# Waiting transfers between the early loads of a fused attention and expert kernel

## The chip, the cores and the metric

One core of one Trainium2 chip. The metric is the device time of one execution in microseconds (us), the median of three runs. SyncE (SP in the profile) issues every transfer of this kernel. TensorE is PE (its weight loads PEld), VectorE is DVE, ScalarE is ACT, GpSimd is POOL.

## The reference

Sliding-window attention, then a dense four-expert layer, then one gated two-layer block:

```python
scores = scale * np.matmul(q, k.transpose(0, 1, 3, 2))       # 2 batches, 8 heads, 576 positions, 64 wide
scores = np.where(masks, scores, -1e9)                       # window 32, plain or with stride 4
attn = softmax(scores); attn_out = attn @ v                  # -> x, 1152 x 512
for e in range(4):
    h = np.maximum(x @ w1[e], 0.0)                           # 512 -> 1024
    out += p[:, e:e + 1] * (h @ w2[e])                       # 1024 -> 512
h = out @ w_in; g = h * sigmoid(1.702 * h); return g @ w_out # 512 -> 2048 -> 512
```

## The kernel before

All products run on PE in two parts, a rounded upper part and the rest, so each weight block is loaded, rounded by ACT (`w_hi`, L199) and its rest taken by DVE or POOL (`w_lo`, L207) before PE can use it.

The first 90 us, attention together with the first expert's first two-thirds, are one hand-ordered list of steps, the string `SCRIPT`. The program runs through it once and emits each step's instructions; every engine then works through its own instructions in that order, each waiting for what it needs. The attention is cut into 16 parts (4 head pairs, times a big and a small range of positions in each of two batches); a big part has two groups and a small one has one, which makes groups 0 to 7 (big, first batch), 8 to 15 (small) and 16 to 23 (big, second batch). The steps that matter here:

- `L j` loads part j's queries and keys (`load_qk`, L243; part 3 comes in two halves), `K j` its values (`load_v`, L253). The tiles are `qkT..` and `v..`.
- `W s w` loads a 512 KB weight block into one of four staging tiles `st` (`w_load`, L184): `W 0 0`, `W 1 0`, `W 3 0`, `W 2 0` for the first product, `W 0 1`, `W 1 1` and so on for the second. `H s w` is the rounding on ACT, `O s w` the rest.
- `S` are the scores on PE (L321), `Q` the masked minimum on DVE (L329), `A` the exponential on ACT (L334), `N` the division (L357), `U` the turn of the probabilities on PE (L365) and `c` its copy, `V` the product with the values (L439).
- `T`, `t`, `r` are, for later groups, the turn by way of a store to HBM (`spill`, L382) and a load of it (`fetch`, L388). These transfers are SyncE's too.
- `F`, `G` are pieces of the first product of expert 0 (L547), `h` and `l` its two output parts, `2` the second product (L577 to L579).

SyncE holds 8 completion semaphores for transfers and uses them in turn: the ninth transfer is issued only once the first has landed. Beside that a load waits only for its tile to be free. After the script, SyncE goes on with the weights of experts 0 to 3 and of the last block, in a schedule of its own, until 605 us.

Of the kernel before, what the change touches and what calls it, by code (L numbers as in the profile page):

```python
# [7 lines left out]
F32 = mybir.dt.float32  # L8
# [7 lines left out]
P = 128  # L16
# [4 lines left out]
S, D, J, NPAIR = 576, 64, 144, 4  # L21
# [51 lines left out]
QK_AT, V_AT = places()  # L73

SCRIPT = """
L 2, P 8, M, L 3 0, L 3 1, S 4, L 1, L 0, Q 4, S 5 6, Q 5, Q 6, W 0 0, L 11, A 4, S 7, A 5, S 2 3, N 4 V, U 4, S 0,
K 2, Q 7, N 5 P, Q 3, A 6, A 7, L 7, L 10, K 3, L 9, K 9, S 1, Q 2, A 2, U 5, W 1 0, N 6 P, L 5, L 6, L 8, N 7 p,
c 4 v, L 4, c 5 a, U 6, Q 1, Q 0, H 0 0 0, c 6 a, A 3, N 2 P, A 1, U 7, O 0 0 p 0, S 15 11, c 7 v, Q 11, K 0, V 5,
V 7, C 5 v, O 0 0 p 1, C 7 v, U 2, F 1 0 1, R 5, c 2 a, H 1 0 0, R 7, N 3 V, K 11, K 1, W 3 0, G 0 2 h, N 1 P,
F 1 1 2, F 0 1 2, S 14 13, F 1 5 6, F 0 4 5, O 1 0 v 0, Q 15, Q 14, W 2 0, K 4, A 0, H 1 0 1, U 3, F 1 4 5, O 1 0 p 1,  # L80
Q 13, F 2 0 1, N 0 V, F 3 0 1, F 0 5 6, c 3 a, H 0 0 1, W 0 1, F 2 4 5, F 2 5 6, S 9 8, U 1, A 11, O 0 0 p 2,
O 0 0 p 3, Q 9, F 3 4 5, c 1 a, Q 8, F 2 1 2, U 0, c 0 a, F 3 1 2, V 3, N 11 p, V 1, A 14, O 1 0 v 3, H 3 0 0, C 3 v,
S 10 12, C 1 v, F 3 5 6, R 3, G 0 1 h, R 1, O 1 0 p 2, H 2 0 0, A 15, F 1 2 3, Q 10, G 1 1 h, F 1 7 8, U 11, H 3 0 1,
O 2 0 v 1, O 2 0 v 0, N 15 v, c 11 v, F 2 7 8, F 3 2 3, T 15, O 3 0 p 1, Q 12, H 2 0 1, L 13, O 3 0 p 3, F 3 6 7,
O 2 0 p 2, F 1 6 7, F 3 7 8, A 9, W 1 1, F 4 4 5, F 7 5 6, F 2 6 7, F 4 1 2, D, O 3 0 p 2, O 2 0 p 3, O 3 0 v 0, L 12,
F 2 2 3, G 0 0 l, F 2 3 4, F 7 3 4, L 15, G 0 0 h, H 0 1 0, O 0 1 p 1, K 10, H 0 1 1, H 1 1 0, L 14, F 5 4 5, F 0 7 8,
F 4 2 3, F 4 6 7, F 6 6 7, h 1, F 6 7 8, F 5 1 2, h 0, l 0, h 2, F 5 6 7, F 7 1 2, t 15, K 5, A 8, A 13, O 1 1 v 1,
l 1, F 5 0 1, F 7 4 5, O 0 1 v 0, F 5 7 8, F 6 4 5, F 5 2 3, F 6 2 3, O 0 1 v 3, W 2 1, W 3 1, N 14 V, l 2, F 5 5 6,
O 0 1 p 2, H 1 1 1, A 12, N 13 V, T 14, F 7 2 3, F 7 0 1, F 5 3 4, 2 0 1, F 4 7 8, 2 1 1, F 6 1 2, 2 0 0, F 6 3 4,
t 14, F 3 3 4, 2 0 2, 2 1 2, F 7 7 8, h 5, 2 1 0, F 7 6 7, O 1 1 v 2, T 13, N 8 P, O 1 1 v 0, h 3, 2 2 2, l 3, t 13,  # L90
O 1 1 p 3, N 9 P, H 2 1 0, A 10, H 2 1 1, F 4 3 4, F 4 0 1, T 8, 2 2 0, F 4 5 6, N 12 V, T 9, 2 3 2, 2 2 1, O 2 1 p 0,
H 3 1 0, F 6 0 1, h 7, N 10 V, O 2 1 p 3, T 12, r 14, l 5, h 4, O 3 1 p 1, 2 3 0, 2 3 1, F 6 5 6, l 7, S 20 22, l 4,
O 2 1 p 1, T 10, S 23 21, h 6, Q 20, Q 23, 2 4 1, t 8, K 7, 2 4 2, A 23, V 11, H 3 1 1, r 15, Q 22, l 6, r 13, V 15,
V 13, O 3 1 p 0, O 2 1 p 2, C 15 a, A 20, t 9, t 10, V 14, N 23 V, 2 5 2, T 23, C 14 v, 2 4 0, C 13 a, r 9, 2 5 0,
2 5 1, N 20 p, K 8, O 3 1 v 3, 2 6 2, O 3 1 p 2, C 11 v, R 13, R 11, T 20, S 18 19, S 16 17, V 9, R 14, Q 21, r 8,
R 15, Q 18, A 21, w, Q 16, K 6, V 8, C 9 v, 2 6 1, 2 6 0, r 10, t 12, t 20, C 8 a, r 12, t 23, K 15, K 12, A 18, R 9,
2 7 2 a, Q 17, R 8, 2 7 1 a, F 9 5 6, F 9 1 2, Q 19, F 10 0 1, 2 7 0 v, F 10 4 5, F 11 4 5, V 10 12, C 10 v,
F 11 1 2, F 9 4 5, F 10 5 6, F 9 0 1, C 12 v, R 10, F 8 6 7, R 12, N 21 v, F 10 3 4, F 11 3 4, r 23, F 8 0 1, F 8 5 6,
F 11 6 7, F 8 2 3, F 13 4 5, F 8 7 8, T 21, B 17 p, F 8 1 2, F 9 3 4, F 8 3 4, F 8 4 5, F 13 0 1, F 11 0 1, B 22 p,
X 22, Y 22, X 17, t 21, F 9 2 3, A 16, F 9 7 8, F 11 2 3, F 10 2 3, h 8, A 19, F 10 7 8, F 10 1 2, F 9 6 7, F 13 5 6,  # L100
N 22 v, F 10 6 7, h 9, h 10, F 11 7 8, T 22, F 13 1 2, F 11 5 6, F 12 4 5, l 8, Y 17, 2 8 1, F 12 2 3, N 16 P,
F 15 0 1, 2 8 2, l 9, T 16, N 18 v, F 12 3 4, 2 9 1, t 22, r 20, F 13 6 7, K 13, 2 9 2, F 15 5 6, F 12 1 2, F 14 1 2,
r 21, h 11, l 10, T 18, l 11, F 12 0 1, F 12 5 6, F 12 6 7, F 13 2 3, F 15 1 2, F 12 7 8, N 17 p, 2 10 1, N 19 p,
r 22, K 14, t 16, T 19, F 13 3 4, t 19, T 17, F 15 3 4, h 12, t 17, F 14 3 4, 2 11 1, F 13 7 8, l 12, t 18, 2 8 0,
F 14 6 7, F 14 0 1, 2 9 0, V 21, V 23, C 23 a, r 17, C 21 a, F 15 2 3, 2 10 0, h 13, R 21, F 14 7 8, l 13, F 14 2 3,
2 12 1, F 15 7 8, R 23, r 19, r 18, F 14 5 6, 2 10 2, 2 11 2, F 15 4 5, 2 12 2, F 15 6 7, 2 11 0, F 14 4 5, r 16,
h 15, h 14, V 19, V 17, 2 12 0, 2 13 1, C 17 v, 2 13 0, l 14, C 19 v, 2 13 2, R 17, l 15, R 19
"""


# [1 line left out]
def fused_kernel(ctx: ExitStack, tc: tile.TileContext, qk, v, dp, w1, w2, w_in, w_out, out):  # L112
# [17 lines left out]
    nc = tc.nc  # L130
# [3 lines left out]
    C = 384  # L134
# [15 lines left out]
    dram = ctx.enter_context(tc.tile_pool(name="dram", bufs=1, space=bass.MemoryType.DRAM))  # L150
# [25 lines left out]
    wst = {}  # L176

    def w_load(s, which):
        if which == 0:
            t = stg.tile([P, KT, 2 * P], F32, tag="stg", name=f"st1_{s}")  # L180
        else:
            t = stg.tile([P, 2, DM], F32, tag="stg", name=f"st2_{s}")
        src = (w1, w2)[which][s].rearrange("p (a b) -> p a b", a=t.shape[1]) if s < 4 * E else late[s - 4 * E, which]
        nc.sync.dma_start(out=t, in_=src)  # L184
        wst[s, which] = t
# [8 lines left out]
    def w_hi(s, which, halves=range(2)):  # L194
        if halves[0] == 0:
            w_tiles(s, which)
        for i in halves:
            half = slice(2 * i, 2 * i + 2) if which == 0 else slice(i, i + 1)
            nc.scalar.activation(wt[s, which][0][:, half, :], wst[s, which][:, half, :], AF.Copy)  # L199
# [29 lines left out]

    qkT = {}  # L230
    vt = {}

    PLACE = {(0, "big"): 0, (0, "small"): 384, (1, "small"): 576, (1, "big"): 768}

    def load_qk(b, pr, kind, half=None):

        off, w, _, _ = QK_AT[b, pr, kind]
        assert half is None or (b, pr, kind) == FIRST_PART
        if (b, pr, kind) not in qkT:
            qkT[b, pr, kind] = ap_.tile([P, 896], F32, tag="qkT", bufs=9, name=f"qkT{b}{pr}{kind}")  # L240
        src = qk[off:off + P * w].rearrange("(p w) -> p w", w=w)
        a, z = (0, w) if half is None else HALVES[half]
        nc.sync.dma_start(out=qkT[b, pr, kind][:, a:z], in_=src[:, a:z])  # L243

    def load_v(b, pr, kind):

        off, w = V_AT[b, pr, kind]
        t = ap_.tile([P, 768], F32, tag="v", bufs=6, name=f"v{b}{pr}{kind}")
        src = v[off:off + P * w].rearrange("(p w) -> p w", w=w)
        if (b, pr, kind) == BESIDE:  # L250
            nc.sync.dma_start(out=t[P // 2:, :w], in_=src[:P // 2])
        else:
            nc.sync.dma_start(out=t[:, :w], in_=src)  # L253
        vt[b, pr, kind] = t[:, :w].rearrange("p (x h d) -> p x h d", h=2, d=D)

    def keep(eng, out, in_):
# [272 lines left out]
    def g1_part(e, c, f, kt, terms):  # L529

        if (c, f) not in part:
            early_bank = e == 0 and c == 0 and f < NTI
            pool, tag = (pacc, f"pa{KT - 1 - f}") if early_bank else (ps, "ps")
            part[c, f] = [pool.tile([P, 512], F32, tag=tag, name=f"g1_{e}{c}{f}"),
                       {(k, x) for k in range(KT) for x in "hl"}]
        pt, todo = part[c, f]
        s, o = divmod(f, 2)
        wh, wl = wt[4 * e + s, 0]
        fs = slice(o * P, (o + 1) * P)
        products = {"h": [(wh, xh), (wl, xh)], "l": [(wh, xl)]}  # L540
        for x in terms:
            if (kt, x) not in todo:
                continue
            first = len(todo) == 2 * KT
            todo.remove((kt, x))
            for y, (w, xx) in enumerate(products[x]):
                nc.tensor.matmul(pt[:, :C], w[:, kt, fs], xx[:, kt, c * C:(c + 1) * C], start=first and y == 0,  # L547
                                 stop=not todo and y == len(products[x]) - 1)
# [430 lines left out]
    def second2(s, c, slots):  # L979
# [25 lines left out]

    seq = [("e", 0, c, f) for c in range(NC) for f in range(F1)]

    steps.update({
        "M": masks,
        "P": spin,  # L1010
        "G": lambda f, i, terms: g1_part(0, 0, f, ORDER[i], terms),
        "W": w_load,
        "H": lambda s_, which, *halves: w_hi(s_, which, list(halves) or range(2)),
        "O": lambda s_, which, eng, *pieces: w_lo(s_, which, list(pieces), {"p": nc.gpsimd, "v": nc.vector}[eng]),
        "F": lambda it, a_, b_: g1_some(*seq[it][1:], TERMS[a_:b_]),
# [251 lines left out]
```

## Time and profile before

| | |
|---|---|
| median of 3 runs | 608.67 us (608.64 to 608.78) |
| the profiled execution | 608.31 us, of which its span is 606.5 us |
| PE, busy in the span | 600.5 us (99%) |
| DVE, ACT, POOL busy | 451.8, 273.1, 318.1 us |
| transfers | 73.31 MB; 39.3% of 16 transfer engines' time |

The span runs from the first instruction to the last one's end; 1.8 us lie around it. A share of busy time is an average over stages: the transfers keep all 16 engines busy until about 30 us and about half of them or less later. A wait in the profile is idle time of an engine before an instruction, with what ended it.

### The profile page before, as it was taken

What the parts mean: (1) busy time and instruction counts of PE and PEld (TensorE: products, weight loads), DVE (VectorE), ACT (ScalarE), POOL (GpSimd) and SP (SyncE); (2) the same over time, 40 slices, a digit from 0 to 9 for tenths busy, and PEclk for the clock granted to TensorE, in tenths of its full rate; (3) what the DMA queues carried; (4) which work ended last, traced back from release to release, by engine and by line L of the source; (5) the groups of instructions that cost most, each with busy time, mean ns of one, the idle gap of its engine ahead of it and who ended that gap; (6) DMA issues with size and microseconds to landing.
All of it is one profiled execution on the core that took longest, in us unless ns stands there. A gap on an engine that the chain in (4) does not pass through costs nothing.

```text
span 606.5 us, 10633 instructions
## 1 busy us (share of the span) xinstructions
PE 600.5 (99%) x3889; PEld 541.1 (89%) x3889; DVE 451.8 (74%) x937; ACT 273.1 (45%) x618; POOL 318.1 (52%) x304
## 2 busy tenths in 40 slices
PE   8999999999999999999999999999999999999997
PEld 5888988999989989998998899999899988988996
DVE  6867625957887887887878689798886766667565
ACT  7965311354535544445355233356464344344321
POOL 5652204764776775866777442385519564473210
PEclk9999999999999999999999999999999999999999
DMA  8954561040764755656553309822003121100004
GB/s 331 367 187 120 154 188 45 0 136 39 225 185 146 226 172 159 192 173 180 184 150 129 109 6 212 167 102 85 21 1 105 35 70 36 35 2 2 0 1 156
DMA packets 55348, 73.31 MB, mean 121 GB/s; under 512 B 26336, under 2 KB 36480, under 8 KB 55296
## 3 DMA queue, kind: packets, MB, share of 16 engines
q1 hardware_dynamic: 55296, 72.64, 39.3%
q8 instruction: 30, 0.49, 0.3%
q14 instruction: 22, 0.18, 0.1%
HBM read 57.03 MB, written 15.59 MB: 120 GB/s over the span
## 4 chain that ended last, share of the span: by engine, by line
PE 96%; DVE 2%; ACT 1%; issue 0%; POOL 0%; DVEq 0%; ACTq 0%; POOLq 0%
PE gd L817 10%; PE gc L817 10%; PE ga L817 10%; PE g L547 8%; PE q L908 7%; PE q L907 7%; PE q L906 7%; PE q L992 5%; PE q L990 5%; PE q L991 5%; PE gb L817 5%; PE pa L577 3%; PE pa L578 3%; PE pa L579 3%; PE q L964 1%; PE q L962 1%
## 5 line engine op out<-in xcount | busy, mean ns | idle before, releaser
L757 POOL TENSOR_TENSOR m<-m,sd 128x512 int32<-128x512 int32 x32 | 47.6, 1488 | 59.3 <-issue 33.5
L912 DVE SCALAR_TENSOR_TENSOR acc<-q,pwe,acc 128x512 f32<-128x512 f32 x81 | 59.9, 747 | 23.9 <-PE q L908 23.7
L701 POOL TENSOR_TENSOR wsl<-ss,wsh 128x512 fp32r<-128x512 f32 x39 | 55.4, 1426 | 38.5 <-ACT wsh L700 28.2
L908 PE MATMUL q<-w2h,h 128*128 128x512 f32 x180 | 70.8, 393 | 0.0
L906 PE MATMUL q<-w2h,h 128*128 128x512 f32 x180 | 70.3, 391 | 0.0
L907 PE MATMUL q<-w2l,h 128*128 128x512 f32 x180 | 70.3, 391 | 0.0
L839 POOL TENSOR_TENSOR cc<-s,u 128x256 f32<-128x256 f32 (+1 forms) x28 | 24.7, 882 | 74.8 <-DVE s L836 74.8
L828 ACT ACTIVATE s<-ga 128x256 f32<-128x256 f32 (+1 forms) x40 | 16.3, 409 | 96.2 <-PE ga L817 96.2
L992 PE MATMUL q<-w2h,h 128*128 128x512 f32 (+1 forms) x146 | 56.9, 390 | 0.0
L990 PE MATMUL q<-w2h,h 128*128 128x512 f32 (+1 forms) x146 | 56.7, 388 | 0.0
L991 PE MATMUL q<-w2l,h 128*128 128x512 f32 (+1 forms) x146 | 56.6, 387 | 0.0
L712 POOL TENSOR_TENSOR w2l<-st,w2h 128x512 fp32r<-128x512 f32 x37 | 50.1, 1367 | 9.8 <-ACT w2h L711 9.3
L999 DVE SCALAR_TENSOR_TENSOR acc<-q,acc 128x512 f32<-128x512 f32 (+1 forms) x64 | 42.4, 677 | 11.5 <-PE q L992 11.2
L697 POOL TENSOR_TENSOR wal<-st,wah 128x512 fp32r<-128x512 f32 (+1 forms) x38 | 40.9, 1082 | 12.3 <-ACT wah L696 12.3
L817 PE MATMUL ga<-xh,wal 128*128 128x256 f32 (+1 forms) x160 | 47.3, 295 | 0.0
L817 PE MATMUL ga<-xh,wah 128*128 128x256 f32 (+1 forms) x160 | 47.2, 295 | 0.0
L817 PE MATMUL ga<-xl,wah 128*128 128x256 f32 (+1 forms) x160 | 47.2, 295 | 0.0
L864 DVE TENSOR_TENSOR h<-cc,h 128x256 fp32r<-128x256 f32 (+3 forms) x40 | 35.1, 877 | 9.2 <-ACT h L861 5.7
L908 PEld LDWEIGHTS q<-w2h,h 128*128 128x128 f32 x180 | 33.8, 188 | 7.3
L907 PEld LDWEIGHTS q<-w2l,h 128*128 128x128 f32 x180 | 33.8, 188 | 6.9
L906 PEld LDWEIGHTS q<-w2h,h 128*128 128x128 f32 x180 | 33.8, 188 | 6.5
L834 DVE TENSOR_TENSOR u<-gb,s 128x256 f32<-128x256 f32 (+1 forms) x40 | 18.2, 455 | 28.4 <-PE gb L817 28.4
(374 smaller groups left out, 1823.4 us busy)
## 6 DMA issues: line engine op xcount, KB each, us to landing
st<-in_w_dram SPq DMA_DIRECT2D x32, 512.0 KB, 5.0
sd<-in_w_in_dram SPq DMA_DIRECT2D x16, 512.0 KB, 4.4
sd<-in_w_out_dram SPq DMA_DIRECT2D x16, 512.0 KB, 4.0
w<-m SPq DMA_DIRECT2D x32, 256.0 KB, 4.6
st<-w SPq DMA_DIRECT2D x16, 512.0 KB, 3.7
out_dram<-acc SPq DMA_DIRECT2D x8, 256.0 KB, 2.0
turned<-acc SPq DMA_DIRECT2D x4, 320.0 KB, 6.7
acc<-turned SPq DMA_DIRECT2D x4, 320.0 KB, 5.2
```

The lines of the kernel that those rows point to most:

```text
L547: nc.tensor.matmul(pt[:, :C], w[:, kt, fs], xx[:, kt, c * C:(c + 1) * C], start=first and y == 0, stop=not todo and y == len(products[x]) - 1)
L701: fns.append(lambda x=x, dst=dst: engine(f"p.{s}.{x}").tensor_tensor(out=sl[:, dst], in0=sums[:, dst], in1=sh[:, dst].bitcast(F32), op=ALU ...
L712: fns.append(lambda o=o: engine(f"q.{s}.{2 * o + 1}").tensor_tensor(out=lo[:, o], in0=t[:, o], in1=hi[:, o].bitcast(F32), op=ALU.subtract))
L757: nc.gpsimd.tensor_tensor(out=m.bitcast(I32), in0=m.bitcast(I32), in1=t.bitcast(I32)[:, :, 0], op=ALU.add)
L817: nc.tensor.matmul(bank_[:, :n], wz[:, y, m, :], xz, start=start and m == 0 and z == 0, stop=m == 1 and z == 2, skip_group_check=not start)
L906: nc.tensor.matmul(pt, hi, wh[:, o, :], start=o == 0, stop=False)
L907: nc.tensor.matmul(pt, hi, wl[:, o, :], start=False, stop=False)
L908: nc.tensor.matmul(pt, lo, wh[:, o, :], start=False, stop=o == 1)
L912: nc.vector.scalar_tensor_tensor(to, pt, pwe[:, s // NF, t:t + 1], dst, op0=ALU.mult, op1=ALU.add)
L990: nc.tensor.matmul(pt, hi, wh[:, o, cols], start=o == 0, stop=False)
L991: nc.tensor.matmul(pt, hi, wl[:, o, cols], start=False, stop=False)
L992: nc.tensor.matmul(pt, lo, wh[:, o, cols], start=False, stop=o == 1)
```

## The change

A new step `J n` is put at fourteen places of the script. It issues a transfer of one number, from the tile that was loaded n loads ago (counted by a new list `newest`, to which `load_qk`, `load_v` and the script's `W` append) into a small HBM tile `seen`, a new column each time. The transfer reads the loaded tile, so SyncE waits until that load has landed before it issues it, and issues nothing behind it until then. No load is taken away, added, or moved against another one.

```diff
+    seen = dram.tile([1, 64], F32, name="seen")
+    newest = []
+
+    def landed(n):
+
+        x = len(newest)
+        nc.sync.dma_start(out=seen[:, x:x + 1], in_=newest[-n])
...
         nc.sync.dma_start(out=qkT[b, pr, kind][:, a:z], in_=src[:, a:z])
+        newest.append(qkT[b, pr, kind][:1, a:a + 1])
...
             nc.sync.dma_start(out=t[:, :w], in_=src)
+        newest.append(t[P // 2:P // 2 + 1, :1])
...
+    def first_load(s_, which):
+        w_load(s_, which)
+        newest.append(wst[s_, which][:1, 0, :1])
...
-        "W": w_load,
+        "W": first_load,
+        "J": landed,
```

The loads of the script with the new steps between them (all other steps left out; t and r are stores and loads by way of HBM):

```
L 2, L 3 0, L 3 1, L 1, L 0, J 5, W 0 0, L 11, J 4, K 2, L 7, L 10, J 5, K 3, L 9, K 9, W 1 0, J 4, L 5, L 6, L 8, L 4,
J 5, K 0, K 11, K 1, W 3 0, J 5, W 2 0, K 4, J 3, W 0 1, L 13, J 4, W 1 1, D, J 3, L 12, J 3, L 15, K 10, J 4, L 14,
t 15, K 5, W 2 1, J 4, W 3 1, t 14, t 13, ..., t 8, J 3, K 7, ..., K 8, ..., K 6, ..., K 15, K 12, ..., J 6, K 13, ...
```

Before, the list is the same without the `J`s.

## Rows read from the trace of the kernel before

**Rows 1.** Waits of PE until 12 us: total us, times, longest.
```profile
PE ppt01big L365 <- POOL prob01big L357: 1.0, 2, 0.5
...
PE s01big L321 <- DMA qkT01big<-in_qk_dram: 0.4, 1, 0.4
```

**Rows 2.** Waits of PE from 12 to 606 us, the only row.
```profile
PE gd L817 <- DVE s L836: 0.3, 1, 0.3
```

**Rows 3.** Chain that ended last, until 25 us: start us, us, what.
```profile
5.22 2.26 ACT prob00big L334 x12
7.47 2.16 ACT prob01big L334 x12
```

**Rows 4.** Timeline of SP: issue start us, us that issuing took.
```profile
3.03 0.43 SPq L184 DMA_DIRECT2D st<-in_w_dram  x1
...
5.72 0.44 SPq L253 DMA_DIRECT2D v01big<-in_v_dram  x1
...
8.89 0.33 SPq L184 DMA_DIRECT2D st<-in_w_dram  x1
...
11.46 0.33 SPq L243 DMA_DIRECT2D qkT02small<-in_qk_dram  x1
...
14.99 1.82 SPq L184 DMA_DIRECT2D st<-in_w_dram  x2
...
15.82 0.99 SPq L184 DMA_DIRECT2D st<-in_w_dram  x1
...
20.49 0.33 SPq L184 DMA_DIRECT2D st<-in_w_dram  x1
...
23.46 0.33 SPq L184 DMA_DIRECT2D st<-in_w_dram  x1
...
28.53 2.63 SPq L382 DMA_DIRECT2D home11small<-tr11small  x4
```

**Rows 5.** Transfers of Rows 4 until 23.46, in its order: KB, us from issue to landing.
```profile
st<-in_w_dram SPq DMA_DIRECT2D x1, 512.0 KB, 5.8
...
v01big<-in_v_dram SPq DMA_DIRECT2D x1, 384.0 KB, 6.7
...
st<-in_w_dram SPq DMA_DIRECT2D x1, 512.0 KB, 6.1
...
qkT02small<-in_qk_dram SPq DMA_DIRECT2D x1, 320.0 KB, 7.2
...
st<-in_w_dram SPq DMA_DIRECT2D x1, 512.0 KB, 6.8
...
st<-in_w_dram SPq DMA_DIRECT2D x1, 512.0 KB, 7.2
...
st<-in_w_dram SPq DMA_DIRECT2D x1, 512.0 KB, 5.1
...
st<-in_w_dram SPq DMA_DIRECT2D x1, 512.0 KB, 4.6
```

**Rows 6.** Single loads issued at 121.75, 41.83, 31.27 and 86.17: KB, us to landing.
```profile
st<-in_w_dram SPq DMA_DIRECT2D x1, 512.0 KB, 3.6
...
v00small<-in_v_dram SPq DMA_DIRECT2D x1, 192.0 KB, 2.6
...
v03small<-in_v_dram SPq DMA_DIRECT2D x1, 256.0 KB, 2.8
...
st<-in_w_dram SPq DMA_DIRECT2D x1, 512.0 KB, 14.5
```

**Rows 7.** Timeline of ACT and PE: the first use of four loads, start us, us.
```profile
15.47 0.61 ACT L199 ACTIVATE wh<-st 128x512 fp32r<-128x512 f32 x1
...
23.43 0.62 ACT L199 ACTIVATE wh<-st 128x512 fp32r<-128x512 f32 x1
...
28.55 0.62 ACT L199 ACTIVATE wh<-st 128x512 fp32r<-128x512 f32 x1
...
19.18 0.29 PE L321 MATMUL s02small<-qkT02small 64*64 64x96 f32 x1
```

## What the change should do to the time, before it was run

> **What bounds the kernel now.** I read the page's busy shares first, but a PE that is busy 99% of the span says little about a change in the first 30 us. So the next view is PE's waits, in two stretches. Until 12 us PE waits for the second half of the keys of the first parts (0.4 us) and for POOL's division, twice (1.0 us) [rows 1]. From 12 us to the end one wait of 0.3 us is left [rows 2]. The reader is to see that PE's queue is full from 12 us on: whatever makes PE wait there is paid in full, and whatever ends sooner there pays nothing unless PE's own work does. The third view is the chain of work that ended last: from 5.22 to 9.63 us it runs on ACT's exponentials, 12 and 12 instructions with no gap (5.22 + 2.26 = 7.48, and the second group starts at 7.47) [rows 3]. POOL's division stands behind them. So the 1.0 us are the price of ACT's work, not of a load.
>
> That leaves the loads as a possible cost only. The fourth view, SyncE's timeline, gives the time of issue, and the view of DMA issues gives the time from there to landing. The landings follow in the order of issue: 8.8 (W 0 0, 3.03 + 5.8), 12.4 (K 3), 15.0 (W 1 0), 18.7 (L 4), 21.8 (W 3 0), 23.0 (W 2 0), 25.6 (W 0 1), 28.1 (W 1 1) [rows 4, 5]. A 512 KB block issued alone lands in 3.6 us and a load of 192 KB in 2.6 us [rows 6]. So a load that takes 6 or 7 us stands behind others for most of it. First uses come soon after the landings: W 1 0 is rounded at 15.47 (0.5 us later), L 4 is needed at 19.18 (0.5), W 2 0 at 23.43 (0.4), W 1 1 at 28.55 (0.45) [rows 7]. These are the margins that the change can eat.
>
> **The change, part by part.** *Removed:* nothing. *Added:* fourteen transfers of one number. The trace before has no such transfer. Its issue costs SyncE at least the 0.33 us of the shorter issues and at most the 0.99 us of the longest single one [rows 4]; I take 0.33 plus 0.07 for the wake-up and the step to the next issue, the gap between rows that follow each other closely, so 0.4 us, and 14 x 0.4 = 5.6 us of SyncE's time. No compute engine takes part, so this is not on PE's path by itself. It would be if a load, store or fetch behind it became late.
>
> *Moved:* everything behind a J waits for its landing. Each J is issued when the n-th last load lands, so the next load goes out 0.4 us after that, and each further load 0.47 us later. I compare the shift of the issue with the time that the load had stood in the queue before (its time to landing less 3.6 us, or less between 2.6 and 3.6 us for a smaller one). If the queue serves in order, a load shifted by less than that lands when it did before.
>
> - W 1 0: the J ahead of K 3 waits for W 0 0, 8.8; K 3 goes out at 9.25, W 1 0 three loads later at 10.7. Shift 10.7 - 8.89 = 1.8; stood 6.1 - 3.6 = 2.5. Not late, 0.7 to spare.
> - L 4: the J waits for K 3, 12.4; L 5 at 12.8, L 4 at 14.2. Shift 2.7; stood at least 7.2 - 3.6 = 3.6. Not late, 0.9 to spare.
> - W 3 0: the J waits for W 1 0, 15.0; it is the fourth load behind it, out at 16.8. Shift 1.8; stood 6.8 - 3.6 = 3.2. Not late.
> - W 2 0: the J waits for L 4, 18.7; out at 19.1 instead of 15.82. Shift 3.3; stood 7.2 - 3.6 = 3.6. Not late, 0.3 to spare, the narrowest.
> - W 0 1: the J waits for W 3 0, 21.8; out at 22.2 instead of 20.49. Shift 1.7; stood 5.1 - 3.6 = 1.5. Late by 0.2.
> - W 1 1: the J waits for W 2 0, 23.0; out at 23.4, as before (23.46). It lands behind W 0 1, so 28.1 + 0.2 = 28.3, against its use at 28.55: 0.25 left.
>
> All from [rows 4 to 7]. The first two holds (J 5 ahead of W 0 0, J 4 ahead of K 2) wait for the first and the fourth load and leave four and three loads in the queue behind these, about as the third and fourth do; I count them as those. Behind W 1 1 come L 12, L 15, K 10 and L 14, for the big groups of the second batch, which the script scores and multiplies some hundred steps later. The J ahead of L 14 waits for W 1 1 (28.3), so the first store t 15 goes out near 29.1 instead of 28.53 [rows 4], 0.6 us late. The last three J's (ahead of W 3 1, K 7 and K 13) wait for loads that landed long ago and cost SyncE 0.4 us each. No wait of PE behind 12 us has a store or fetch as its releaser [rows 2], so such a lateness has some cover; how much, that row doesn't say.
>
> What a transfer of one number does to the queue is bounded from both sides. Low end: a 256 KB load issued right behind four stores to HBM (t 15) landed in 2.8 us, against 2.6 us for 192 KB with little ahead, so small writes to HBM ahead of it cost nothing that can be seen. High end: the queue stands for the whole time of a single small transfer, at most 2.6 us [rows 6]. Between them lies the block issued at 86.17, just ahead of 1152 single numbers written to HBM (L1061): 14.5 us, of which 3.6 us are its own and three blocks ahead of it are 3 x 1.2 (21.8 to 23.0 for one block [rows 4, 5]). The rest, 7.3 us, is 6 ns a number, or 0.1 us where 16 engines share them. The case is nearest to this one, numbers of 4 bytes in HBM: I take 0.1 us, and six of them ahead of W 2 0 add 0.6 us to the 0.3 to spare, which would still be about its margin of 0.4.
>
> The Trainium skill (DMA: Bandwidth & Descriptors, Anatomy of one DMA) speaks against this change: it gives every transfer about 2.0 us of fixed cost, most of it the wait for the receipt of the last write, heaviest when the target is HBM. If that time held the queue, the sum by that page would be 6 x 2.0 - 0.4 = 11.6 us, an estimate; if only the small transfer's own landing waits for it, it would be nothing, since nothing waits for that landing.
>
> **The sum.** Removed 0; on PE's path 0, covered by the queue that the loads stand in and by the 0.25 us left at W 1 1. The profiled execution (608.31 us, 606.5 in the span and 1.8 around it) stays, and it lies 0.36 under the median of the runs, 608.67. Forecast 608.7 us. The measurement can tell about 0.2% from no change, 1.2 us here.
>
> **Rivals.**
>
> *The queue runs dry at each hold (slower).* Place: the six holds ahead of W 2 0. If each leaves the transfer engines without work for g us, W 2 0 lands 6g late, and ACT, and then PE behind it, is late by 6g - 0.4. This decides from g = (1.2 + 0.4) / 6 = 0.27 us; with g = 0.5 it is 2.6 us, 611.3; the middle of the two is 610.6. For it: the spare time at W 2 0 is 0.3 and at W 0 1 it is negative, and an issue sometimes takes 0.6 us longer than others (0.99 against 0.33, and 2.63 for four) [rows 4]. Against it: the holds before have 0.7 us and more to spare. Chance 0.15.
>
> *Each small transfer holds the queue (slower).* Price: by the high end 6 x 2.6 - 0.4 = 15.2 us, 623.9; it decides from 0.27 us each, as above. For it: the 14.5 us block; against it: the load behind four stores [rows 6]. Chance 0.04.
>
> *The early loads land sooner (faster).* With W 0 0 and what follows held back, the keys of the first parts have the transfer engines to themselves, and both waits of rows 1 go: 0.4 + 1.0 = 1.4 us, 607.3. For it: a load wait is there. Against it: ACT's chain from 5.22 us starts before that half of the keys is used and has no gap [rows 3], so PE, 0.4 us sooner, would wait 0.4 us longer for POOL; and the first load of all has nothing held back ahead of it. Chance 0.05.
>
> *The change doesn't do what it says.* At most 8 transfers are under way as it is, and a J takes one of those places itself; the loads' landings stay, and so does the time, 608.7. It differs from the forecast in SyncE's timeline alone. Chance 0.06.
>
> **How the numbers follow.** No change by either of two ways: 0.70 + 0.06 = 0.76. Slower: 0.15 + 0.04 = 0.19. Faster: 0.05. The likeliest alone spans 608.2 to 609.4 (half a us of gain at the first wait, or the 0.25 us at W 1 1 overdrawn). The range reaches into the first rival to its middle, 610.6, and leaves out its upper part, the queue that stands, and the faster case: 608.2 to 610.6.
>
> **What would show it.** Right: SyncE's issues of W 1 0, W 2 0 and W 0 1 near 10.7, 19.1 and 22.2 us; their times to landing down to about 4 us with the landings where they were; PE's waits behind 12 us still some 0.3 us in all. Wrong: landings of W 1 0, L 4 or W 2 0 more than 0.5 us later, and ACT waiting for them (dry queue); gaps of 2 us in the landings behind each J (queue held); PE's wait for POOL gone from before 12 us (faster). I would also be wrong if a late store or fetch reached PE later in the script, which the rows can't exclude.

## The result, and the profile after

The changed kernel takes 612.25 us (median of 6 runs, 610.75 to 613.87) against 608.81 us for the kernel before (6 runs, 608.64 to 609.23): a ratio of 1.0056, with a 95% interval of 1.0045 to 1.0067. It is slower by 3.4 us and lies above the forecast range. These runs spread over 3 us, those of the kernel before over 0.6 us.

The profiled execution took 611.87 us with a span of 610.1 us, 3.6 us more than before. PE's busy time rose by 1.0 us (600.5 to 601.5) and its idle time by 2.6 us (6.0 to 8.6). The first view is PE's waits in the changed kernel, from 12 us to the end (total us, times, longest):

```profile
PE pv01big L449 <- DMA v01big<-in_v_dram: 0.8, 1, 0.8
PE s00small L331 <- DMA qkT00small<-in_qk_dram: 0.6, 1, 0.6
PE s02small L331 <- DMA qkT02small<-in_qk_dram: 0.5, 1, 0.5
PE pv00small L449 <- DMA v00small<-in_v_dram: 0.3, 1, 0.3
PE gd L827 <- DVE s L846: 0.3, 1, 0.3
PE pv01small L449 <- DVE prob11big L367: 0.2, 1, 0.2
```

Before, the `gd` row stood alone [rows 2]. Four of the five new rows name a load: values of parts K 3 and K 7, keys of L 7 and L 4. They sum to 2.2 us, all five to 2.4 us. Until 12 us PE waits as long in sum as before, though for other things: 1.5 us for `qkT03big` and 0.2 us for POOL's division, together 1.7 us; before, it was 1.0 and 0.4 us [rows 1] and 0.3 us for DVE.

PE's timeline shows where it falls behind. The start of the first product on each of four tiles, before and then after (`s02small` before is in [rows 7]):

```profile
11.84 0.29 PE L321 MATMUL s00small<-qkT00small 64*64 64x96 f32 x1
...
13.24 0.87 PE L439 MATMUL pv01big<-pT01big,v01big 96*64 96x64 f32 x24
...
49.00 0.52 PE L439 MATMUL pv01small<-pT01small,v01small 96*64 96x64 f32 x12
```

```profile
12.74 0.26 PE L331 MATMUL s00small<-qkT00small 64*64 64x96 f32 x1 [0.61 <-DMA qkT00small<-in_qk_dram]
...
15.15 0.92 PE L449 MATMUL pv01big<-pT01big,v01big 96*64 96x64 f32 x24 [0.85 <-DMA v01big<-in_v_dram]
...
20.87 0.38 PE L331 MATMUL s03small<-qkT03small 64*64 64x96 f32 x2
21.74 0.27 PE L331 MATMUL s02small<-qkT02small 64*64 64x96 f32 x1 [0.50 <-DMA qkT02small<-in_qk_dram]
...
52.24 0.57 PE L449 MATMUL pv01small<-pT01small,v01small 96*64 96x64 f32 x12 [0.15 <-DVE prob11big L367]
```

PE is 0.9 us late at L 7's keys, 1.9 at K 3's values, 2.6 at L 4's keys (21.74 against 19.18) and 3.2 us at 52 us. Most of the 1.0 us more busy time belongs to the same waits: before, the scores on `s03small` and `s02small` start together (19.17 and 19.18); now two products on `s03small` run alone for 0.38 us, and the rest waits with `s02small`. The same happens at `s00small`, some 0.4 us each.

The second view is SyncE's timeline of the changed kernel, issue start and length. A `seen` row starts when the load that it names has landed, so these rows give the landings too:

```profile
7.21 0.24 SPq L239 DMA_DIRECT2D seen<-qkT03big  x1
7.50 0.34 SPq L262 DMA_DIRECT2D v00big<-in_v_dram  x1
...
9.51 0.24 SPq L239 DMA_DIRECT2D seen<-st  x1
9.80 0.34 SPq L262 DMA_DIRECT2D v01big<-in_v_dram  x1
...
11.13 0.43 SPq L185 DMA_DIRECT2D st<-in_w_dram  x1
15.08 0.24 SPq L239 DMA_DIRECT2D seen<-v01big  x1
15.37 0.34 SPq L251 DMA_DIRECT2D qkT03small<-in_qk_dram  x1
...
17.36 0.24 SPq L239 DMA_DIRECT2D seen<-st  x1
...
21.67 0.24 SPq L239 DMA_DIRECT2D seen<-qkT02small  x1
21.95 0.34 SPq L185 DMA_DIRECT2D st<-in_w_dram  x1
...
27.26 0.24 SPq L239 DMA_DIRECT2D seen<-st  x1
27.59 0.34 SPq L185 DMA_DIRECT2D st<-in_w_dram  x1
```

Against [rows 4, 5]: K 3 (`v01big`) lands at 15.1 instead of 12.4 us, W 1 0 at 17.4 instead of 15.0, L 4 (`qkT02small`) at 21.7 instead of 18.7, W 2 0 at 27.3 instead of 23.0. They are late by 2.7, 2.4, 3.0 and 4.2 us. The third view is the busy time of the engines in three stretches, first of the kernel before, then of the changed one; the columns are PE, PEld, DVE, ACT and POOL with their instructions, the granted clock, the transfer engines' busy share (packet times added up, so it can pass 1) and GB/s:

```profile
6.00:14.00 8.00, 6.68 (x126) 5.29 (x120) 7.61 (x62) 8.00 (x42) 4.37 (x9) 1.00 1.04 399
14.00:22.00 8.00, 7.88 (x105) 6.61 (x103) 6.72 (x47) 7.05 (x30) 4.45 (x9) 1.00 1.04 387
22.00:34.00 12.00, 12.00 (x123) 11.76 (x118) 10.84 (x39) 11.80 (x48) 7.49 (x12) 1.00 0.89 305
```

```profile
6.00:14.00 8.00, 5.82 (x88) 4.49 (x90) 6.59 (x60) 8.00 (x42) 4.70 (x10) 1.00 0.98 316
14.00:22.00 8.00, 6.66 (x100) 5.65 (x98) 5.53 (x30) 6.26 (x27) 3.70 (x8) 1.00 0.84 292
22.00:34.00 12.00, 12.00 (x151) 11.35 (x143) 8.46 (x47) 8.68 (x30) 6.82 (x11) 1.00 0.87 295
```

From 6 to 22 us the changed kernel moves 8 x (316 + 292) = 4.9 MB instead of 8 x (399 + 387) = 6.3 MB. The missing 1.4 MB are 3.6 us at the 393 GB/s of before, a little more than the 3.0 us by which L 4 landed late near 22 us. That this equals the growth of the span is in part chance: PE was 2.6 us late by then, L 4's lateness less the 0.5 us that its first use had stood behind the landing [rows 5, 7], and lost the rest later. For K 3 the same sum is 2.7 less 0.85 us (landing at 12.4, first use at 13.24). ACT's rounding now waits too, where it had no such wait, but no row of PE's waits names it; from the whole list of ACT's waits until 40 us:

```profile
ACT wh L200 <- DMA st<-in_w_dram: 2.1, 3, 1.1
```

### The profile page after: what moved, and what is told of

It reads as the page before. It is cut to its first block, busy times and chain, and to the rows that moved or that the text cites. A ratio compares the mean times of both kernels' runs of the same rounds, so it can differ in the third digit from the quotient of the medians.

```text
span 610.1 us, 10647 instructions
## 1 busy us (share of the span) xinstructions
PE 601.5 (99%) x3889; PEld 541.7 (89%) x3889; DVE 451.4 (74%) x937; ACT 273.6 (45%) x618; POOL 318.3 (52%) x304
## 4 chain that ended last, share of the span: by engine, by line
PE 94%; DMA 3%; DVE 2%; issue 1%; ACT 0%; SPq 0%; POOL 0%; DVEq 0%; ACTq 0%
PE gd L827 10%; PE gc L827 10%; PE ga L827 10%; PE g L557 8%; PE q L918 7%; PE q L917 7%; PE q L916 7%; PE q L1002 5%; PE q L1000 5%; PE q L1001 5%; PE gb L827 5%; PE pa L587 3%; PE pa L588 3%; PE pa L589 3%; PE q L972 1%; PE q L974 1%
```

## Experiments

The theories. **A:** a hold leaves too little in the queue; until the next loads are issued and running, the transfer engines lose time, and everything behind is late. **B:** the fourteen small transfers cost it themselves. **C:** the later holds make the stores and fetches by way of HBM late. **D:** a wait of SyncE at these places costs, whatever it leaves under way. Each ratio is to the kernel before in the same comparison, with its 95% interval; in us it is worked out on 608.7.

**Without a hold.**

```diff
-    const.tile([P, 8], F32, name="pad")
+    pad = const.tile([P, 8], F32, name="pad")
+    nc.vector.memset(pad, 0.0)
...
-        nc.sync.dma_start(out=seen[:, x:x + 1], in_=newest[-n])
+        nc.sync.dma_start(out=seen[:, x:x + 1], in_=pad[:1, :1])
```

> Same fourteen transfers of one number at the same places, but each reads a tile that is written once at the start, so SyncE waits for no load. Theory A (the hold lets the transfer engines run dry, and the loads behind it come late): the loss of 3.4 us goes, 608.5 to 609.4 us. Rival B (the small transfers themselves cost it: 0.4 us of SyncE's issue each, a number written to HBM in the queue, one of the eight places under way): the time stays at 611 to 613 us.

Measured: 609.42 us, ratio 1.0009 (1.0000 to 1.0018), 0.5 us, at the upper edge of A's range. The fourteen transfers at their places cost 0 to 1.1 us; the waits cost the rest. B can hold at most that share. SyncE isn't free of waits here: each small transfer takes one of its 8 places, so K 3 goes out at 8.48 us instead of 5.72, and W 0 1 lands at 27.7 instead of 25.6. Loads that go out late while the others are still under way cost little here.

**The number into SBUF.** `pad` is a tile that nothing else uses.

```diff
-    const.tile([P, 8], F32, name="pad")
+    pad = const.tile([P, 8], F32, name="pad")
+    seen = pad[:1, :]
...
-    seen = dram.tile([1, 64], F32, name="seen")
...
-        nc.sync.dma_start(out=seen[:, x:x + 1], in_=newest[-n])
+        nc.sync.dma_start(out=seen[:, x % 8:x % 8 + 1], in_=newest[-n])
```

> The holds as in the changed kernel, but the number goes into an unused SBUF tile instead of HBM. Theory A: no difference, 611 to 613.5 us. Rival B in its form that the write to HBM holds the queue: 609 to 610 us.

Measured: 613.86 us, ratio 1.0085 (1.0072 to 1.0099). Neither expectation: the write to HBM isn't what costs, but the kernel became slower still, by 0.3% beyond the changed one. SyncE's timeline of this kernel shows a possible reason:

```profile
6.86 0.60 SPq L239 DMA_DIRECT2D pad<-qkT03big  x1
7.50 0.38 SPq L262 DMA_DIRECT2D v00big<-in_v_dram  x1
...
9.74 0.59 SPq L239 DMA_DIRECT2D pad<-st  x1
10.37 0.38 SPq L262 DMA_DIRECT2D v01big<-in_v_dram  x1
```

The issue of the number takes 0.60 us instead of 0.24 us, so each hold is some 0.35 us longer. Six early holds would make 2.1 us, and 1.8 us were measured (5.2 - 3.4), but the two needn't be the same: W 2 0 lands at 28.1, only 0.8 us later than in the changed kernel, and PE has a wait of 1.3 us for DVE that the changed kernel doesn't have. So a longer hold is a likely part of it and not shown as the whole; why this issue takes longer stays open.

**The first six holds, and the last eight.** The script keeps only those `J` steps.

> Only the first six of the fourteen holds (until ahead of W 2 0). Theory A: the four waits of PE for loads until 22 us and so nearly the whole loss stay, 611 to 613 us. Rival C (the holds behind 22 us make the stores and fetches by way of HBM late, and PE pays there): 609 us, the loss goes with the other eight.

> Only the last eight holds (from ahead of W 0 1). Theory A: the loads that PE waited for land as before the change; W 0 1 and W 1 1 may be a us late, so 608.7 to 609.7 us. Rival C: 611 to 612 us.

Measured: 610.94 us, ratio 1.0035 (1.0022 to 1.0048), for the first six; 608.89 us, ratio 1.0004 (0.9995 to 1.0013), for the last eight. The early holds carry most of it, 2.1 us, just below the expected range; the late ones alone can't be told from no change. C falls as the main cause, though its path exists: in the profile of the last eight alone PE waits 0.6 us for a fetch:

```profile
PE pv01small L450 <- DMA pT01small<-home01small: 0.6, 1, 0.6
```

**Two loads deeper, one load less.** The first hold stays as it is in the deeper version, since only five loads are issued by then.

```diff
 # deeper: J 5, J 4, J 5, J 4, J 5, J 5, J 3, ...
+ J 5, J 6, J 7, J 6, J 7, J 7, J 5, ...
 # one less:
+ J 4, J 3, J 4, J 3, J 4, J 4, J 2, ...
```

> The fourteen transfers, each but the first reading the tile two loads further back, so that two more loads stay under way at each hold. Theory A (the queue runs dry at a hold): the work left in the queue grows by about 1 to 1.5 us a hold, more than the 0.7 us that a hold lost, so 608.8 to 609.8 us, the price of the transfers without a hold. Rival D (any wait of SyncE at these places costs, however many loads are under way): 611 to 612 us.

> Each hold with one load less under way than in the changed kernel. Theory A: each of the six early holds leaves some 0.5 to 1 us less work in the queue, all of it lost time, so 3 to 6 us more than the changed kernel, 615 to 618 us. Rival D: 612 to 613 us, as the changed kernel.

> The changed kernel again, beside the others on one chip: 611 to 613.5 us, its own spread; every theory expects the same.

Measured on one chip: deeper 609.70 us, ratio 1.0012 (1.0003 to 1.0021); as changed 612.36 us, 1.0054 (1.0040 to 1.0067); one less 615.98 us, 1.0109 (1.0094 to 1.0123). The time follows what is left under way, 0.7, 3.3 and 6.6 us, with the same fourteen waits in all three. D falls. The first two of the same three stretches for the deeper version, then for one load less:

```profile
6.00:14.00 8.00, 6.33 (x110) 4.95 (x108) 7.01 (x64) 8.00 (x42) 4.31 (x9) 1.00 1.00 365
14.00:22.00 8.00, 7.58 (x110) 6.38 (x107) 7.40 (x37) 6.58 (x28) 4.68 (x9) 1.00 1.03 357
```

```profile
6.00:14.00 8.00, 6.31 (x100) 4.79 (x94) 7.57 (x66) 8.00 (x41) 3.63 (x8) 1.00 0.86 299
14.00:22.00 8.00, 6.71 (x98) 5.66 (x92) 5.82 (x34) 6.96 (x31) 5.09 (x10) 1.00 0.87 283
```

The same two stretches for the changed kernel on this chip, and for the kernel without a hold:

```profile
6.00:14.00 8.00, 6.01 (x82) 4.49 (x84) 6.29 (x57) 8.00 (x42) 4.24 (x9) 1.00 0.98 335
14.00:22.00 8.00, 6.94 (x104) 5.99 (x107) 6.04 (x34) 6.47 (x27) 4.35 (x9) 1.00 0.99 333
```

```profile
6.00:14.00 8.00, 7.13 (x128) 5.71 (x128) 7.23 (x62) 8.00 (x43) 4.70 (x10) 1.00 1.00 373
14.00:22.00 8.00, 7.67 (x98) 6.47 (x95) 6.24 (x42) 6.58 (x28) 4.25 (x8) 1.00 1.00 332
```

On this chip the rate orders as the times do: 365 and 357 GB/s, 335 and 333 (changed), 299 and 283. It is a rough measure all the same: the changed kernel itself gave 316 and 292 in its first profile, and the kernel without a hold, only 0.5 us slower than before, falls to 332 in the second stretch.

**The second hold alone, and the same hold one load deeper.** `J 4` ahead of `K 2` as the only hold, and then `J 5` there.

> Only the second hold (ahead of K 2). Theory A with the loss at the first load behind the hold: K 2, L 7 and L 10 land some 1 us late, and because the transfer engines have no idle time until 17 us the loads after them do too, W 1 0 more than its 0.5 us to spare: 609.3 to 610.2 us. If the loss needs the holds to add up: 608.6 to 609.0 us.

> The second hold alone, but reading the load before (L 3 1 instead of L 1), so that K 2 goes out about 1 us sooner than with the second hold alone. Theory A, with the loss where the first load behind a hold has no time to spare: K 2 now has about 1.2 us to spare, so the loss of 1.4 us goes, 608.9 to 609.6 us. If one hold costs about 1.4 us whatever it leaves under way: 610.5 us.

Measured: 610.53 us, ratio 1.0026 (1.0015 to 1.0038), a little above its range, and 609.03 us, ratio 1.0008 (0.9999 to 1.0017). SyncE's timeline around the hold, `J 4` first and `J 5` second:

```profile
6.85 0.29 SPq L239 DMA_DIRECT2D seen<-qkT03big  x1
7.19 0.36 SPq L262 DMA_DIRECT2D v00big<-in_v_dram  x1
```

```profile
5.82 0.30 SPq L239 DMA_DIRECT2D seen<-qkT01big  x1
6.16 0.35 SPq L262 DMA_DIRECT2D v00big<-in_v_dram  x1
```

One hold is enough for 1.6 us, and sending K 2 out 1.0 us sooner takes that back to what can't be told from no change. With `J 4` alone PE waits 1.8 us for `v01big`, a load that no hold stands directly ahead of: the loss is passed down the queue. The stretch from 9 to 12 us, before and with `J 4` alone:

```profile
9.00:12.00 3.00, 1.98 (x22) 1.19 (x24) 2.83 (x23) 3.00 (x15) 1.66 (x4) 1.00 1.03 396
```

```profile
9.00:12.00 3.00, 2.08 (x22) 1.47 (x20) 2.84 (x23) 3.00 (x17) 2.03 (x4) 1.00 0.84 226
```

By 9 us K 2 and three more loads had been issued behind the hold, and still the rate is little over half of before until 12 us. So the loss isn't only the time in which nothing is issued; why the rate comes back so late stays open.

**All but the second, and the fourth alone.**

> Thirteen holds, without the second. If the losses of the single holds add up, some 1.4 us of the 3.3 us go: 610.5 to 611.3 us. If what one hold loses is given back by the next (the next hold then has less work to wait for): 612 us, as with all fourteen.

> The fourth hold alone (ahead of L 5, waiting for K 3). Theory A by the same reckoning as for K 2: L 5 is shifted by 3.4 us and had stood about 3.4 us, no time to spare, so a loss like the second hold's but nearer to its users: 609.3 to 610.5 us. If the second hold is special because the transfer engines are only just started: 608.8 to 609.2 us.

Measured: 611.63 us, ratio 1.0047 (1.0034 to 1.0059), and 609.54 us, ratio 1.0014 (1.0005 to 1.0023). The fourth hold (ahead of L 5) costs 0.9 us by itself, so the second isn't special. But the second's 1.6 us don't come off when it is taken out of fourteen: 2.9 us are left of about 3.3, between the two expectations. The two intervals overlap, so the times alone don't settle it, but the landings do for one load: K 3 lands at 16.1 us with the second hold alone and at 15.1 with all fourteen. The losses of single holds don't simply add up.

No version beat the kernel before, and none was expected to: PE's only waits for loads there are the 0.4 us ahead of ACT's chain [rows 1, 3].

## Why the prediction was wrong

The forecast was no change; what came is nearest to the rival in which the queue runs dry at each hold, by another path than it gave. Step by step:

- *PE is full from 12 us on, so lateness is paid and nothing can be gained.* Right: the loss is in PE's waits for loads behind 12 us, 2.2 us, with the rest in one more wait for DVE and in 1.0 us more busy time, most of it scores that a late load held up. Until 12 us ACT's chain hid the waits for loads: 1.5 us for `qkT03big` came, most of the 1.0 us for POOL went, and the sum stayed 1.7 us.
- *The margins of 0.4 to 0.5 us at the first uses.* Right for L 4, where PE waited. But PE waited first for L 7 and K 3, which the list of margins leaves out (0.95 and 0.85 us: landings at 10.9 and 12.4, first uses at 11.84 and 13.24). And ACT's margin at a weight block isn't PE's: W 2 0 landed 4.2 us late, its margin at ACT was 0.4, PE was 2.6 us late from its own waits, and still no row of PE's waits names ACT.
- *The spare time at each hold.* **This is the step that failed.** I reckoned it at the last load behind the hold (W 1 0: 0.7 us, L 4: 0.9 us) and put the second hold down as "those". But the loads go out 0.47 us apart after the hold, and before the change K 3 and the next three loads had taken 3.2 us to go out, 1.06 us apart (5.72 to 8.89 [rows 4]), so the shift is largest at the first load. By the same rule for a load of 384 KB (3.2 us alone, between the 2.6 and 3.6 us of [rows 6]): K 3 goes out at 9.25 instead of 5.72, a shift of 3.5 us, and had stood 6.7 - 3.2 = 3.5 us. Nothing is spare. The same for K 2 gives a shift of 3.0 against 3.2. The chain of estimates had no room for a single late landing, and the measured issue times left it at once: K 3 at 9.80 (reckoned 9.25), L 5 at 15.37 (12.8), W 2 0 at 21.95 (19.1). Even so reckoned the rule is too kind, since it would still have K 3 land about on time. It lets a load behind a hold land in the time that it takes alone, 3.2 us; K 3 took 5.3 us (9.80 to 15.08), with K 2, L 7 and L 10 ahead of it, late themselves. K 2 took 5.0 us in the run with the second hold alone. In place of spare time the changed kernel showed landings 2.4 to 4.2 us late, from K 3 on. The sum's 0 on PE's path rested on this spare time; it measured 3.4 us.
- *The rival's formula.* W 2 0 came 4.2 us late behind six holds, so g = 0.7 us, and 6g - 0.4 = 3.8 us against 3.4 to 3.6 measured. The mechanism and its point of decision (g = 0.27 us) stood in the text; its chance was set from the margins of the wrong loads. That the number comes out near is partly luck. The formula goes by W 2 0, ACT and then PE, and PE's waits name K 3, L 7 and L 4 instead. The losses aren't equal either: K 3 is 2.7 us late behind three holds, W 2 0 4.2 behind six; the second hold alone costs 1.6 us, the fourth alone 0.9, the first six together 2.1.
- *The price of a small transfer.* 0.1 us in the queue was assumed; without a hold, fourteen cost 0.5 us (0 to 1.1), under 0.1 us each. SyncE's step from the start of a small issue to the next one took 0.29 us (7.21 to 7.50) instead of 0.4. The Trainium skill (DMA: Bandwidth & Descriptors, Anatomy of one DMA) gives a transfer about 2.0 us of fixed cost, in a section on transfers that GpSimd issues. Here SyncE issued them, and that time did not hold the queue: the fourteen without a hold cost 0.5 us.
- *Stores and fetches.* A late fetch or store isn't the main cause (last eight holds alone: 1.0004). In that run's profile a fetch does reach PE late, by 0.6 us, as the prediction said it couldn't exclude. The 0.3 us wait for `v00small` stands behind the thirteenth hold (0.8 us when the changed kernel ran again), and the last eight alone don't show a loss that can be measured.

## What to carry to other kernels

Where transfers are busy without a gap and their first uses follow within a us, holding loads back gains nothing and must leave enough under way to cover the whole way from a landing until the next loads run at full rate. Reckon that at the first load behind the hold, since it is shifted most, and at every load behind it that has a user close by; expect any shortfall to be passed to everything behind it. When such an estimate comes out at zero to spare, the dry case is the forecast and not the rival.

## What the hardware showed that was not expected

- The missing rate is only in part idle transfer engines. From 6 to 14 us the busy share fell from 1.04 to 0.98 but the rate from 399 to 316 GB/s: 384 GB/s for a full share before, 322 after. From 14 to 22 us it was 372 and 348. It isn't peculiar to the waits: without a hold it was 332 GB/s at a share of 1.00. Counted from the traces' packet records between 6 and 22 us, most packets take as long as ever, and a few take over twice the usual time of their size: 17 of 2487 before, 84 of 2052 in the changed kernel, 59 of 2284 without a hold. What holds these up is open.
- Issuing a transfer of one number takes SyncE 0.24 to 0.30 us in the changed kernel, where it goes to HBM, and 0.58 to 0.72 us when it goes to SBUF.
- Whether the changed kernel repeats less well is open: 610.75 to 613.87 us over its first 6 runs against 608.64 to 609.23 for the kernel before, but 611.89 to 612.58 over 5 against 608.28 to 609.51 over 19 when it ran again. The second hold alone, beside these, gave 609.02 to 612.90 over 9.
